# Laying out anew the filler products of a kernel's last four modes

## The chip, the cores and the metric

The kernel runs on one core of one Trainium2 chip. The metric is the time of one execution on the device, in microseconds (us); lower is better. Times below are medians of several executions.

Engine names in the profile: PE stands for the matrix products (2551 `MATMUL` records in the kernel before), PEld for the loads of their stationary operand (as many `LDWEIGHTS`), DVE and ACT for the vector and scalar engines; POOL and SP here mostly start DMA transfers (161 of POOL's 165 records are `DMA_DIRECT2D`). "PEclk" is the clock granted to PE, as a share of the full one. L340 is line 340 of the kernel. In the changed kernel lines from 381 on stand two lower, so L404 before is L406 after.

## The reference

A linear attention forms `x`. A spectral mix then takes the first 64 Fourier modes of `x` along the sequence, multiplies each mode by its own complex 512x512 matrix and transforms back. A channel product with a rectifier ends it:

```python
X  = np.fft.rfft(x, axis=1)                       # x: (8, 576, 512)
Yr = einsum(Xr, w_r) - einsum(Xi, w_i)            # per mode m: "bmd,mde->bme", 64 modes
Yi = einsum(Xr, w_i) + einsum(Xi, w_r)
y  = np.fft.irfft(Y, n=S, axis=1)
u  = x + y
out = u + np.maximum(u @ w_ch, 0.0)
```

What matters for the time: each mode has two weight matrices (`wr`, `wi`), 128 in all, which are loaded once and used once.

## The kernel before

The weights come in mode by mode. Each mode `kk` multiplies `wr`, then `wi` into a PSUM tile `P`; DVE or ACT casts `P` to `ys`; four small products turn it into `yt`. In the last four modes (60 to 63) *fillers* are put in: products of the identity with part of `wch16` into a PSUM tile that nobody reads before it is overwritten. They only keep PE at work. `pin` fixes the order in the program.

```python
    def w_load(kk, half, pool, tag, bufs):
        # ... the last weight, wi of mode 63, comes in two transfers: 3/4 and 1/4
        for dcs in (slice(0, 3), slice(3, 4)) if (kk, half) == (NM - 1, 1) else (slice(0, NDC),):
            tc.keep_in_program_order(nc.gpsimd.dma_start(out=w[:, dcs], in_=rows_of[:, dcs, :]))

    def keep_warm(n):
        for _ in range(n):
            pin(nc.tensor.matmul(last_ps[0], id16, wch16[:, 0, :]))      # 128x512, L340

    def mode_product(kk, ps, stage, yt_ps):
        # ...
        for t, w in ((1, wr), (0, wi)):
            # ... four products of 32 columns each, side by side, into P           (L355)
            if t == 1 and kk >= NM - 4:
                keep_warm(6)                       # first place: between wr and wi
        if NM - 4 <= kk < NM - 1:
            keep_warm(3)                           # second place: while P is cast
        # ... ys = cast of P: DVE in even modes (L369), ACT in odd ones (L371)
        # ... yt = four products of ys with pick_sb                                (L373)
        if NM - 4 <= kk < NM - 1:
            keep_warm(3)                           # third place: after yt

    def last_mode(ps):                             # mode 63, 16 products per weight (L393)
        # ...
        product(1, wr, range(NDC))
        keep_warm(3)
        product(0, wi, range(3))
        product(0, wi, range(3, NDC))
        nc.vector.tensor_copy(out=YT[:, :, kk, :], in_=y_last)          # "the YT cast", L404
```

After the YT cast come the products `zl` and `ypl` (L674, L684), small transfers into `YZ`, and a tail of inverse products (L549, L593) with the stores of the output.

Of the kernel before, what the change touches and what calls it, by code (L numbers as in the profile page):

```python
# [47 lines left out]
def kernel(  # L48
# [48 lines left out]
    def xt_cols(dc: int, t: int, kk: int):  # L97

        c0 = dc * XDC + t * B * NM + kk
        return xt_c[:, c0 : c0 + 31 * NM + 1 : NM]  # L100
# [231 lines left out]
    def w_get(kk: int):  # L332
        if kk not in w_in:
            w_in[kk] = [w_load(kk, half, wpool, "w", W_KEEP) for half in range(2)]
        return w_in.pop(kk)

    def keep_warm(n: int):

        for _ in range(n):
            pin(nc.tensor.matmul(last_ps[0], id16, wch16[:, 0, :]))  # L340

    def mode_product(kk: int, ps, stage, yt_ps):

        wr, wi = w_get(kk)
        st = stage.tile([128, D], F16, tag="ystage", bufs=2, name=f"ys{kk}")

        n_part = 1
        pw = D // n_part
        P = [
            ps.tile([128, D], F32, tag="P", bufs=2, name=f"P{kk}_{i}")[:, 0:pw] for i in range(n_part)  # L350
        ]
        for t, w in ((1, wr), (0, wi)):
            for i in range(n_part):
                for dc in range(NDC):
                    mm = nc.tensor.matmul(  # L355
                        P[i][dc * 32 : dc * 32 + 32, :], xt_cols(dc, t, kk),
                        w[:, dc, i * pw : i * pw + pw],
                        start=(t == 1), stop=(t == 0), tile_position=(0, dc * 32),
                    )
                    if kk >= NM - 4:  # L360
                        pin(mm)
            if t == 1 and kk >= NM - 4:
                keep_warm(6)
        if NM - 4 <= kk < NM - 1:
            keep_warm(3)
        for i in range(n_part):
            dst = st[:, i * pw : i * pw + pw]
            if (kk + i) % 2 == 0:
                nc.vector.tensor_copy(out=dst, in_=P[i])  # L369
            else:  # L370
                nc.scalar.copy(out=dst, in_=P[i])  # L371
        for ec in range(NDC):
            mm = nc.tensor.matmul(  # L373
                yt_ps[:, ec, kk % 8, :], st[:, ec * 128 : ec * 128 + 128], pick_sb
            )
            if kk >= NM - 4:
                pin(mm)
        if NM - 4 <= kk < NM - 1:
            keep_warm(3)

    def last_mode(ps):

        kk = NM - 1
        wr, wi = w_get(kk)
        y_last = ps.tile([128, NDC, 2 * B], F32, tag="P", bufs=2, name="y_last")

        def product(t, w, dcs):
            for dc in dcs:
                c0 = dc * XDC + t * B * NM + kk
                x = xt_c[:, c0 : c0 + (2 * B - 1) * NM + 1 : NM]  # L390
                for ec in range(NDC):
                    pin(
                        nc.tensor.matmul(  # L393
                            y_last[:, ec, :], w[:, dc, ec * 128 : ec * 128 + 128], x,
                            start=(t == 1 and dc == 0 and ec == 0), stop=(t == 0 and dc == NDC - 1),
                            skip_group_check=True,
                        )
                    )

        product(1, wr, range(NDC))  # L400
        keep_warm(3)
        product(0, wi, range(3))
        product(0, wi, range(3, NDC))
        nc.vector.tensor_copy(out=YT[:, :, kk, :], in_=y_last)  # L404
# [23 lines left out]
    def mode(kk: int):  # L428
        nonlocal yt_ps
        if kk % 8 == 0:  # L430
            yt_ps = psW.tile([128, NDC, 8, 2 * B], F32, tag="yt", bufs=1, name=f"yt{kk // 8}")
        if kk == NM - 1:
            last_mode(psW)
            return
        mode_product(kk, psW, ystage, yt_ps)
        if kk == NM - 2:
            nc.vector.tensor_copy(out=YT[:, :, NE : NM - 1, :], in_=yt_ps[:, :, 0 : NL - 1, :])
        elif kk % 8 == 7:
            nc.vector.tensor_copy(out=YT[:, :, kk - 7 : kk + 1, :], in_=yt_ps)
# [299 lines left out]
```

## Time and profile before

The median was 431.39 us of three runs (431.38 to 431.8).

| quantity | value | where it is read |
|---|---|---|
| span of the profiled execution | 429.8 us | page |
| queue of the weights (with q, k and v) | 82 MB, 98.2% of the DMA engines' span | page, queues |
| PE clock | 0.50 or 1.00 by turns, then 1.00 from 364.2 to 425.6 us | windows, clock records |
| fillers | 39 | code, timeline |
| last YT cast starts | 395.68 us | timeline |
| last piece of `wi` of mode 63 lands | 380.74 + 13.8 = 394.5 us | DMA issues |
| YT cast to the end of the span | 34.1 us | 429.77 - 395.68 |

From the page of the kernel before: the rows of the PE's busy share and of its clock in 40 slices of 10.7 us (tenths), the queue of the weights, and the chain that ended last.

```profile
PE   0358776887018776856886666778675758999993
PEclk9999666565558765566556678555658655999998
q0 software_dynamic: 32000, 82.00, 98.2%
DMA 67%; PE 17%; issue 7%; DVE 4%; ACT 2%; POOL 1%; DVEq 0%; POOLq 0%; ACTq 0%
```

Two thirds of the chain is waiting for transfers, 55% for weights (`wi` 33%, `wr` 22% in the page's list by line). PE is mostly under 80% busy until about slice 35, and its clock is low on average. Then the last slices are full and at full clock: PE takes over there. The change lies in that stretch.

From the timeline of the kernel before (start us, duration us, engine, line, operation, out<-in, shape, count, and in brackets the idle time before it with its releaser), mode 60 and then mode 63:

```profile
380.20 1.07 POOL L115 DMA_DIRECT2D wi<-in_moe_w_i_dram  x2
...
382.25 0.47 PE L355 MATMUL P<-wr,xt_c 128*32 128x512 bf16 x4
382.66 1.47 PE L340 MATMUL zl<-wch,id 128*128 128x512 f16 x6
384.06 0.47 PE L355 MATMUL P<-wi,xt_c 128*32 128x512 bf16 x4
384.47 0.82 PE L340 MATMUL zl<-wch,id 128*128 128x512 f16 x3
384.59 0.69 DVE L369 CAST ys<-P 128x512 f16<-128x512 f32 x1 [5.18 <-PE P L355]
385.33 0.26 PE L373 MATMUL yt<-pick_sb,ys 128*128 128x16 f16 x4
385.45 0.81 PE L340 MATMUL zl<-wch,id 128*128 128x512 f16 x3
386.19 0.47 PE L355 MATMUL P<-wr,xt_c 128*32 128x512 bf16 x4
...
393.68 0.73 PEld L393 LDWEIGHTS <-wr 128*128 128x128 bf16 x16
394.36 0.81 PE L340 MATMUL zl<-wch,id 128*128 128x512 f16 x3
394.80 0.73 PEld L393 LDWEIGHTS <-wi 128*128 128x128 bf16 x16
395.68 0.22 DVE L404 CAST YT<-y_last 128x64 f16<-128x64 f32 x1 [1.64 <-PE y_last L393]
395.97 1.05 PE L674 MATMUL zl<-wch,YT 128*128 128x256 f16 x8 [0.32 <-DVE YT L404]
```

No line of PE between 382 and 395 us carries an idle bracket: PE is never waiting for a weight here. The three fillers in the second place (384.47) run in the very time that the DVE cast takes (384.59 to 385.28), before `yt` can start at 385.33. The other fillers are followed at once by the next real product, so they push it back. The first line shows that the last weights were already under way at 380.2 us. From the view of DMA issues of the kernel before, window around 380.7 us (size, us from issue to landing), the two pieces of `wi` of mode 63:

```profile
wi<-in_moe_w_i_dram POOLq DMA_DIRECT2D x1, 384.0 KB, 13.6
wi<-in_moe_w_i_dram POOLq DMA_DIRECT2D x1, 128.0 KB, 13.8
```

Issued at 380.20 and 380.74 us, they land at 393.8 and 394.5 us. PE starts to load that weight at 394.80, so it is 1.0 us late for the first piece.

### The profile page before, as it was taken

Reading aid. Unit: us, or ns where it says so; the run is one execution under the profiler, and the core shown is the slowest. Engines: PE = TensorE matmul, PEld = TensorE weight load, DVE = VectorE, ACT = ScalarE, POOL = GpSimd, SP = SyncE. Lnnn points to the kernel's source line nnn. Section 1 sums busy time; section 2 is a strip of 40 time slices with the busy share of each in tenths; the row PEclk is TensorE's granted clock in tenths of the full one; section 3 lists DMA queues with packets and bytes.
Section 4 is the critical chain, followed back from the end, with each engine's and each line's share of the span. In section 5 each row is a group of like instructions: output and inputs, shape, how many; then the busy total and the mean of one; then the engine's idle time right before and its main releaser. Section 6 shows DMA issues by size and latency. Waiting matters only on the chain.

```text
span 429.8 us, 6238 instructions
## 1 busy us (share of the span) xinstructions
PE 296.9 (69%) x2551; PEld 154.8 (36%) x2551; DVE 181.9 (42%) x373; ACT 146.6 (34%) x227; POOL 91.5 (21%) x165
## 2 busy tenths in 40 slices
PE   0358776887018776856886666778675758999993
PEld 0346555664003332322232222322222324954441
DVE  1699998955004233233232322332323322211694
ACT  3687666631002222222222322122212222311782
POOL 4232223222102312121112221221211121110200
PEclk9999666565558765566556678555658655999998
DMA  8999999999999999999999999999999999995697
GB/s 148 207 208 209 209 210 210 211 214 215 222 211 214 215 213 214 214 214 214 213 213 214 214 213 214 213 214 214 213 213 214 214 214 214 214 213 97 239 369 296
DMA packets 35803, 92.38 MB, mean 215 GB/s; under 512 B 3136, under 2 KB 16448, under 8 KB 35776
## 3 DMA queue, kind: packets, MB, share of 16 engines
q0 software_dynamic: 32000, 82.00, 98.2%
q1 hardware_dynamic: 3776, 10.00, 6.1%
q8 instruction: 20, 0.33, 0.3%
q14 instruction: 7, 0.06, 0.0%
HBM read 164.07 MB, written 9.44 MB: 404 GB/s over the span
## 4 chain that ended last, share of the span: by engine, by line
DMA 67%; PE 17%; issue 7%; DVE 4%; ACT 2%; POOL 1%; DVEq 0%; POOLq 0%; ACTq 0%
DMA wi<-in_moe_w_i_dram 33%; DMA wr<-in_moe_w_r_dram 22%; DMA k<-in_k_dram 11%; PE acc L549 4%; PE P L355 3%; PE z L530 2%; PE zl L340 2%; PE acc L593 2%; PE eps L507 2%; PE yp L534 1%; DVE x L272 1%; ACT ke L187 1%; DVE k L194 0%; ACT qT L223 0%; POOL q L169 0%
## 5 line engine op out<-in xcount | busy, mean ns | idle before, releaser
L507 PE MATMUL eps<-wch,xTw 128*128 128x512 f16 x144 | 62.3, 582 | 3.4 <-DVE xTw L504 3.1
L515 ACT CAST E<-eps 128x512 f16<-128x512 f32 (+1 forms) x40 | 21.3, 543 | 122.7 <-PE eps L507 122.7
L115 POOL DMA_DIRECT2D wr<-in_moe_w_r_dram x64 | 34.0, 531 | 135.5 <-PE P L355 109.4
L355 PE MATMUL P<-wi,xt_c 128*32 128x512 bf16 x252 | 42.1, 565 | 27.3 <-DMA wi<-in_moe_w_i_dram 27.3
L355 PE MATMUL P<-wr,xt_c 128*32 128x512 bf16 x252 | 42.6, 582 | 22.9 <-DMA wr<-in_moe_w_r_dram 20.9
L115 POOL DMA_DIRECT2D wi<-in_moe_w_i_dram x65 | 34.5, 531 | 108.5 <-PE P L355 74.1
L355 PEld LDWEIGHTS <-xt_c 128*32 128x32 bf16 x504 | 24.3, 163 | 67.8 <-issue 38.7
L369 DVE CAST ys<-P 128x512 f16<-128x512 f32 x32 | 22.0, 688 | 59.7 <-PE P L355 59.7
L151 PEld LDWEIGHTS <-qT 64*128 64x128 f16 (+1 forms) x640 | 21.5, 126 | 56.8 <-issue 41.8
L371 ACT CAST ys<-P 128x512 f16<-128x512 f32 x31 | 18.1, 585 | 63.2 <-PE P L355 63.0
L373 PE MATMUL yt<-pick_sb,ys 128*128 128x16 f16 x252 | 16.8, 177 | 31.6 <-DMA pick_sb<-row_pick 20.4
L504 DVE COPY xTw<-xTp 128x512 f16<-128x512 f16 x36 | 15.2, 423 | 51.8 <-PE xTp L502 51.8
L373 PEld LDWEIGHTS <-ys 128*128 128x128 f16 x252 | 12.3, 105 | 51.1 <-issue 23.4
L151 PE MATMUL num<-kv,qT 64*128 64x65 f16 (+1 forms) x320 | 14.0, 230 | 22.6 <-ACT kv L247 20.1
L507 PEld LDWEIGHTS <-xTw 128*128 128x128 f16 x144 | 14.7, 124 | 33.7 <-issue 24.2
L492 DVE TENSOR_TENSOR x_main<-nw,rd 128x256 f32<-128x256 f32 x32 | 12.1, 419 | 33.8 <-PE nw L151 33.7
L187 ACT ACTIVATE qe<-q 128x1152 f16<-128x1152 f16 x16 | 17.7, 1155 | 22.9 <-DMA q<-in_q_dram 22.9
L216 PE MATMUL qTp<-id,qe 128*128 128x128 f16 x144 | 16.6, 310 | 12.1 <-DVE qe L200 11.7
L499 ACT CAST x16w<-x_main 128x512 f16<-128x512 f32 x32 | 19.8, 619 | 14.2 <-DVE x_main L492 14.2
L272 DVE TENSOR_TENSOR x<-num,rd 128x512 f16<-128x512 f32 x32 | 22.1, 691 | 1.1
L491 DVE RECIPROCAL rdw<-nw 128x4 f32<-128x4 f32 (+1 forms) x40 | 5.5, 170 | 38.3 <-PE nw L151 38.2
L502 PE MATMUL xTp<-id,x16w 128*128 128x128 f16 x144 | 19.4, 278 | 2.8 <-ACT x16w L499 2.4
(71 smaller groups left out, 413.7 us busy)
## 6 DMA issues: line engine op xcount, KB each, us to landing
wr<-in_moe_w_r_dram POOLq DMA_DIRECT2D x64, 512.0 KB, 18.6
wi<-in_moe_w_i_dram POOLq DMA_DIRECT2D x63, 512.0 KB, 18.6
out_dram<-x_main SPq DMA_DIRECT2D x14, 512.0 KB, 3.1
q<-in_q_dram POOLq DMA_DIRECT2D x8, 576.0 KB, 13.5
k<-in_k_dram POOLq DMA_DIRECT2D x8, 576.0 KB, 14.7
v<-in_v_dram POOLq DMA_DIRECT2D x8, 576.0 KB, 16.9
out_dram<-x_main SPq DMA_DIRECT2D x4, 256.0 KB, 3.4
out_dram<-x_tail SPq DMA_DIRECT2D x2, 512.0 KB, 3.4
```

What stands on the lines that cost most here:

```text
L115: tc.keep_in_program_order(nc.gpsimd.dma_start(out=w[:, dcs], in_=rows_of[:, dcs, :]))
L151: mm = nc.tensor.matmul(num[hpo][orow, c0 : c0 + 65], qT[rows, hpp, h2, cols], kv_sb[rows, hpp, h2, :])
L187: pin(nc.scalar.activation(out=ev[:, c], in_=heads(nm, b)[:, c], func=AF.Exp))
L272: nc.vector.tensor_tensor(out=dst.rearrange("p (o c d) -> p o c d", o=2, c=4), in0=nv[:, :, :, 0:64], in1=rden.unsqueeze(3).broadcast_to([ ...
L355: mm = nc.tensor.matmul(P[i][dc * 32 : dc * 32 + 32, :], xt_cols(dc, t, kk), w[:, dc, i * pw : i * pw + pw], start=(t == 1), stop=(t == 0) ...
L369: nc.vector.tensor_copy(out=dst, in_=P[i])
L371: nc.scalar.copy(out=dst, in_=P[i])
L373: mm = nc.tensor.matmul(yt_ps[:, ec, kk % 8, :], st[:, ec * 128 : ec * 128 + 128], pick_sb)
L499: nc.scalar.copy(out=x16, in_=x)
L502: nc.tensor.transpose(xT_ps[:, c, :], x16[:, c * 128 : c * 128 + 128], id16)
L507: nc.tensor.matmul(e_ps, xT[:, c, :], wch16[:, c, :], start=(c == 0), stop=(c == NDC - 1))
L515: nc.scalar.copy(out=dst, in_=e_ps[:, cols])
```

## The change

The intent, by its own words: fewer fillers in the first two of the four modes, and more between the last mode's two weight halves. The three numbers of a mode are the three places marked above; 39 fillers become 32.

```diff
             if t == 1 and kk >= NM - 4:
-                keep_warm(6)
+                keep_warm(FILL[kk][0])
         if NM - 4 <= kk < NM - 1:
-            keep_warm(3)
+            keep_warm(FILL[kk][1])
 ...
         if NM - 4 <= kk < NM - 1:
-            keep_warm(3)
+            keep_warm(FILL[kk][2])
+
+    FILL = {60: (3, 1, 1), 61: (5, 2, 2), 62: (6, 3, 3), 63: (6, 0, 0)}
 ...
         product(1, wr, range(NDC))
-        keep_warm(3)
+        keep_warm(FILL[kk][0])
         product(0, wi, range(3))
```

In this form the kernel before is `60, 61, 62: (6, 3, 3), 63: (3, 0, 0)`. The order of instructions on every engine other than PE is the same in both.

## The prediction

> **What bounds the kernel now.** The page's chain is 67% DMA: the stream of weights (98% of the 16 engines' span on the software queue) sets the time up to about 361 us. Windows view and timeline show a switch there: from 361 to 397 us the PE hardly pauses, at full clock (PEclk 1.00 from 364.2 to 425.6 us), first on a backlog (z, yp), then from 382.25 us on modes 60 to 63 with 39 fillers (L340). The chain in this stretch runs through PE, except for casts. DMA issues (start plus time to landing) against the timeline: wr60 377.2, used 382.25; wr61 382.1, used 386.2; wr62 387.0, used 390.1; wr63 392.0, used 393.7; first three quarters of wi63 393.8, used 394.8; last quarter 394.5, used about 395.3. Slack shrinks from 5 to under 1 us.
>
> **What the change does.** Only PE's order changes: ten fillers leave before mode 63 (mode 60: 3, 2, 2; mode 61: 1, 1, 1), three join between wr63 and wi63; 32 remain. Weights are issued before 381 us, ahead of the first filler, so landings should not move. One full-clock 128x512 product costs 0.215 us (chain: four take 0.86).
>
> - The three fillers taken between the wi products and yt are worth nothing: yt waits for the cast (DVE 0.69, ACT 0.58 us, plus handovers; 0.80 to 0.87 us from filler start to yt), longer than three fillers (0.65).
> - The other seven (3+1 before wi, 2+1 after yt) are on the chain: 7 x 0.215 = 1.5 us. Mode 63 then wants wr63 at about 392.2, just after its landing.
> - Three added fillers give back 0.65 us. wi63 is then wanted at about 393.95, its landing 393.8; the last quarter at about 394.45, its landing 394.5. A wait of 0.1 to 0.2 us may appear there.
>
> Net on the critical path: about -0.86 us by PE, at most about -0.8 by the landing of the last quarter; I take -0.7. Everything after should just slide earlier.
>
> **Clock.** [...] In the windows view, full-clock stretches of that length with 1.6 to 1.9 us of PE work are mostly followed by half clock; 2.67 and 2.71 us (377.9 and 394.9 us) are not. The thinned modes keep, by my estimate, at least 2.7 of 3.41 us. So I expect it to hold; lost before the tail, it would cost about 100 inverse products up to 0.2 us each.
>
> **Predicted time: 430.7 us (before 431.39), 80% range 430.1 to 431.6.** Chances: faster by over 2% 0.005, within 2% 0.97, slower by over 2% 0.025.
>
> **What would show it right:** first P product of mode 60 at the same time (about 382.3); mode 61 some 1.1 us earlier, mode 62 about 1.5 earlier; yt in mode 60 after 0.5 us of PE idle released by the cast; wi63 and the first zl (L674) 0.6 to 0.9 us earlier; PEclk still 1.00 up to the last products; the same distance from zl to the end.
>
> **What would make it wrong:** the landing of wr63 or wi63 releasing the last products later than I read (stragglers: DMA share is only 0.15 in the last 1.5 us), which would eat the gain; the clock dropping; a tail set by stores rather than by its start; noise (the runs before span 0.4 us).

The sum: 7 x 0.215 us off and 3 x 0.215 us on are the -0.86 us by PE, the landing makes it -0.8 at most, and -0.7 was taken. The 0.215 us is read from the trace: four products of 512 columns at full clock (L549) take 0.86 us from the first start to the next product's (403.33 to 404.19 us). "That length" is 3.41 us, the step in the windows view. Between 261.8 and 340.3 us five such stretches at full clock held 1.61 to 1.93 us of PE work; four were followed by half clock (1.61, 1.93, 1.76 and 1.83 us), one was not (1.88 us). That the clock would hold with 2.7 us is an inference from these and from the two stretches with 2.67 and 2.71 us. The 2.7 us itself is an estimate. The cost of a lost clock is an estimate too: at half clock four `eps` products of 512 columns took 1.68 us to the next product's start (360.70 to 362.38 us), 0.42 each, which is 0.2 us more than 0.215.

## The result, and the profile after

In the first measurement the changed kernel took 430.85 us (430.51 to 431.29, four runs) against 431.44 us (431.38 to 431.8, four runs). The ratio was 0.9985, with a 95% interval of 0.9968 to 1.0002: within 2%, and by itself not clear of 1. The experiments ran on four different chips, so kernels are compared through the ratio. A ratio is the mean time of one kernel's runs over that of the other's of the same rounds, so it isn't quite the ratio of the medians.

The timeline of the kernel after, the lines that answer to those of before:

```profile
379.46 1.07 POOL L115 DMA_DIRECT2D wi<-in_moe_w_i_dram  x2
...
381.51 0.47 PE L355 MATMUL P<-wr,xt_c 128*32 128x512 bf16 x4
381.92 0.82 PE L340 MATMUL zl<-wch,id 128*128 128x512 f16 x3
382.67 0.47 PE L355 MATMUL P<-wi,xt_c 128*32 128x512 bf16 x4
383.07 0.39 PE L340 MATMUL zl<-wch,id 128*128 128x512 f16 x1
383.20 0.69 DVE L369 CAST ys<-P 128x512 f16<-128x512 f32 x1 [4.53 <-PE P L355]
383.94 0.26 PE L373 MATMUL yt<-pick_sb,ys 128*128 128x16 f16 x4 [0.48 <-DVE ys L369]
384.06 0.38 PE L340 MATMUL zl<-wch,id 128*128 128x512 f16 x1
384.37 0.47 PE L355 MATMUL P<-wr,xt_c 128*32 128x512 bf16 x4
...
391.42 0.73 PEld L395 LDWEIGHTS <-wr 128*128 128x128 bf16 x16
392.10 1.46 PE L340 MATMUL zl<-wch,id 128*128 128x512 f16 x6
393.18 0.82 PEld L395 LDWEIGHTS <-wi 128*128 128x128 bf16 x16
394.16 0.23 DVE L406 CAST YT<-y_last 128x64 f16<-128x64 f32 x1 [2.37 <-PE y_last L395]
394.44 1.05 PE L676 MATMUL zl<-wch,YT 128*128 128x256 f16 x8 [0.32 <-DVE YT L406]
```

The two profiled executions differ by 1.53 us in span (429.77 against 428.24), which is more than the 0.86 us that the prediction gave the change at most. Their runs took 431.88 and 430.51 us, one above the median of its kernel and one below. The timelines split it. Mode 60 starts 0.74 us sooner (381.51 against 382.25), before any filler: that is a difference between executions, not of the kernels (more on it at the end). From there to the YT cast it takes 12.65 us instead of 13.43, 0.78 less: that belongs to the change. From the YT cast to the end of the span it takes 34.08 us against 34.09: nothing.

Inside the 0.78 us, mode 60 to 61 takes 2.86 us instead of 3.94. That is 1.08 less for five fillers in the chain (5 x 0.215 = 1.08), although seven have left. The other two stood in the second place; where they were, there is now a bracket of 0.48 us of idle time that ends with the cast. At the end, loading `wi` takes 0.82 instead of 0.73 us: about 0.1 us of waiting for its last piece.

### The profile page after: what moved, and what is told of

Same layout as the page of the kernel before. It is cut to its first block, busy times and chain, and to the rows that moved or that the text cites. A ratio compares the mean times of both kernels' runs of the same rounds, so it can differ in the third digit from the quotient of the medians.

```text
span 428.2 us, 6224 instructions
## 1 busy us (share of the span) xinstructions
PE 295.5 (69%) x2544; PEld 153.7 (36%) x2544; DVE 182.0 (42%) x373; ACT 146.7 (34%) x227; POOL 91.9 (21%) x165
## 4 chain that ended last, share of the span: by engine, by line
DMA 67%; PE 17%; issue 7%; DVE 4%; ACT 2%; POOL 1%; DVEq 0%; POOLq 0%; ACTq 0%
DMA wi<-in_moe_w_i_dram 33%; DMA wr<-in_moe_w_r_dram 23%; DMA k<-in_k_dram 11%; PE acc L551 4%; PE P L355 3%; PE z L532 2%; PE acc L595 2%; PE eps L509 2%; PE zl L340 2%; PE yp L536 1%; DVE x L272 1%; ACT ke L187 1%; DVE k L194 0%; ACT qT L223 0%; POOL q L169 0%
```

## The experiments

Every experiment is the changed kernel with other numbers in `FILL`, so each diff is one line (against the changed kernel), and all gave right results. Five measurements per profile tell most of it, so they come first as one table. "Mode 60" is the start of its first product, "landing" the issue of the last piece of `wi` of mode 63 plus its time to landing (good to 0.1 us), "YT" the start of the YT cast, all in us of the timeline. "Tail" is the span minus YT. The last two columns are the median of the timed runs and their ratio, not the profiled run alone. "Clock lost" is a stretch with PEclk 0.50 between 366 and 420 us.

| profile | mode 60 | landing | YT | YT - landing | tail | clock lost | time, us | ratio to before (95%) |
|---|---|---|---|---|---|---|---|---|
| before | 382.25 | 394.54 | 395.68 | 1.14 | 34.09 | no | 431.44 | |
| the change, first | 381.51 | 393.80 | 394.16 | 0.36 | 34.08 | no | 430.85 | 0.9985 (0.9968 to 1.0002) |
| same_again | 380.94 | 394.12 | 394.43 | 0.31 | 34.04 | no | 430.81 | 0.9979 (0.9967 to 0.9992) |
| again_b | 381.57 | 394.85 | 395.24 | 0.39 | 34.14 | no | 431.01 | 0.9991 (0.9975 to 1.0006) |
| cast_only | 381.64 | 394.12 | 395.07 | 0.95 | 34.20 | no | 431.89 | 0.9996 (0.9984 to 1.0009) |
| chain_only | 381.67 | 394.25 | 394.58 | 0.33 | 34.14 | no | 430.84 | 0.9979 (0.9966 to 0.9991) |
| add_only | 381.75 | 393.84 | 395.78 | 1.94 | 34.10 | no | 432.30 | 1.0016 (1.0002 to 1.0030) |
| cut_only | 381.20 | 393.69 | 394.03 | 0.34 | 34.18 | no | 431.20 | 0.9996 (0.9980 to 1.0012) |
| cut_d | 380.87 | 393.75 | 394.06 | 0.31 | 34.09 | no | 430.73 | 0.9985 (0.9970 to 1.0001) |
| none | 382.27 | 394.45 | 394.77 | 0.32 | 35.41 | 385.5 to 399.2 | 432.47 | 1.0020 (1.0008 to 1.0032) |
| late_only | 379.60 | 393.79 | 394.83 | 1.04 | 34.25 | 385.0 to 391.8 | 431.45 | 0.9989 (0.9976 to 1.0003) |

Where the last landing is what PE waited for, the YT cast starts 0.31 to 0.39 us after it. Where the number is larger, PE itself came late.

**Theory A**: seven fillers that stand in PE's chain leave and three come; the three in the second place are hidden behind the cast; the landing of the last weight is the floor. **Rivals**: B, the gain is only where the weight stream happened to stand in that run; C, every filler costs its 0.215 us wherever it stands; D, the fillers do nothing for the clock.

### The change itself again (same_again)

No edit.

> The changed kernel once more, in five rounds. D is the distance in the timeline from the first P product of mode 60 to the last YT cast (from y_last): 13.43 us before, 12.65 in the first profile of the change (-0.78). Theory A (seven fillers on PE's chain leave, three come, and the landing of the last quarter of wi63 takes back about 0.1): D again 12.6 to 12.75, ratio of times about 0.998. Rival B (the 0.6 us of the first result is only where the run's weight stream happened to stand): D varies by as much as the time does, and the ratio is within 0.0005 of 1.

The ratio came as A said, 0.9979, with an interval that excludes 1, so rival B falls by its second half. The distance D did not come as A said: it was 13.49 us, 0.84 more than in the first profile, as the first half of B had it. From the timeline of same_again:

```profile
380.94 0.48 PE L355 MATMUL P<-wr,xt_c 128*32 128x512 bf16 x4
...
391.65 0.65 PE L395 MATMUL y_last<-xt_c,wr 128*128 128x16 bf16 x16 [0.27 <-DMA wr<-in_moe_w_r_dram]
393.45 0.94 PE L395 MATMUL y_last<-xt_c,wi 128*128 128x16 bf16 x16
394.43 0.22 DVE L406 CAST YT<-y_last 128x64 f16<-128x64 f32 x1 [3.06 <-PE y_last L395]
```

Here PE reached mode 60 sooner while the weights landed later. PE waited 0.27 us for `wr` and about 0.3 us inside `wi` (0.94 us instead of 0.64), and the YT cast stands 0.31 us after the last landing. So D is not a property of the kernel once the landing binds. The distance from the landing is the better measure, and the table uses it.

### Only the fillers beside the cast leave (cast_only)

```diff
-    FILL = {60: (3, 1, 1), 61: (5, 2, 2), 62: (6, 3, 3), 63: (6, 0, 0)}
+    FILL = {60: (6, 1, 3), 61: (6, 2, 3), 62: (6, 3, 3), 63: (3, 0, 0)}
```

> Only the three fillers that stand between a mode's wi products and its yt products leave (mode 60: two, mode 61: one); 36 remain. Theory A: PE waits for the ys cast there anyway, so D stays 13.43 us (13.35 to 13.5), idle before yt about 0.5 us in mode 60 and 0.2 in mode 61, ratio 1.000. Rival C (every filler costs its 0.215 us): D 12.8, ratio 0.9985.

D was 13.43 us (395.07 - 381.64), as before to the last digit, and the ratio 0.9996 (its interval, from 0.9984, still holds C's 0.9985, so it is the trace that decides). From the timeline of cast_only, the `yt` products of modes 60 and 61:

```profile
384.72 0.26 PE L373 MATMUL yt<-pick_sb,ys 128*128 128x16 f16 x4 [0.48 <-DVE ys L369]
...
388.59 0.26 PE L373 MATMUL yt<-pick_sb,ys 128*128 128x16 f16 x4 [0.20 <-ACT ys L371]
```

The fillers turned into idle time, 0.48 and 0.20 us. Rival C falls.

### All of the change but that (chain_only)

```diff
-    FILL = {60: (3, 1, 1), 61: (5, 2, 2), 62: (6, 3, 3), 63: (6, 0, 0)}
+    FILL = {60: (3, 3, 1), 61: (5, 3, 2), 62: (6, 3, 3), 63: (6, 0, 0)}
```

> The change without its cut between wi products and yt: seven fillers leave elsewhere, three come between wr63 and wi63; 35 remain. Theory A: the same as the change, D 12.65 us (12.55 to 12.75), ratio about 0.998. Rival C: D 0.65 us longer, 13.3, ratio about 0.9995.

The ratio was 0.9979, the same as the change's in the same rounds (medians 430.84 and 430.81 us). D was 12.91 us, above the range that was expected, because the landing bound it: YT came 0.33 us after the landing. From the timeline of chain_only, the last quarter of `wi` and the YT cast:

```profile
394.25 0.17 PEld L395 LDWEIGHTS <-wi 128*128 128x128 bf16 x4 [0.24 <-DMA wi<-in_moe_w_i_dram]
394.58 0.23 DVE L406 CAST YT<-y_last 128x64 f16<-128x64 f32 x1 [2.62 <-PE y_last L395]
```

Rival C predicted 0.9995, outside the interval (0.9966 to 0.9991), and falls here too.

### Only the three added (add_only)

```diff
-    FILL = {60: (3, 1, 1), 61: (5, 2, 2), 62: (6, 3, 3), 63: (6, 0, 0)}
+    FILL = {60: (6, 3, 3), 61: (6, 3, 3), 62: (6, 3, 3), 63: (6, 0, 0)}
```

> Only the three fillers between wr63 and wi63 are added; 42 in all. Theory A: they stand on the chain, no landing hides them (wi63 has landed 1 us before it is used), so D is 13.43 + 0.65 = 14.08 us, ratio about 1.0015. Rival (fillers there are hidden behind the landing of wi63): D stays 13.43, ratio 1.000.

D was 14.03 us, 0.60 more than before, and the ratio 1.0016. From the timeline of add_only, `wi` is loaded without a wait:

```profile
394.94 0.69 PEld L395 LDWEIGHTS <-wi 128*128 128x128 bf16 x16
395.78 0.22 DVE L406 CAST YT<-y_last 128x64 f16<-128x64 f32 x1 [2.23 <-PE y_last L395]
```

Added to a kernel whose PE is late, fillers between `wr` and `wi` cost nearly their full time (three times 0.215 is 0.65). In the change they are nearly free only because the other removals have made PE early.

### Only the ten removed (cut_only, cut_a, cut_b, cut_c, cut_d and again_b)

```diff
-    FILL = {60: (3, 1, 1), 61: (5, 2, 2), 62: (6, 3, 3), 63: (6, 0, 0)}
+    FILL = {60: (3, 1, 1), 61: (5, 2, 2), 62: (6, 3, 3), 63: (3, 0, 0)}
```

> The change's ten removals without its three additions; 29 fillers. Theory A: PE comes to wi63 0.65 us sooner than in the change but must wait for its landing: the first three quarters land about 0.7 us before the last one, so PE idles about 0.5 us before wi63 and again before its last quarter; D 12.55 to 12.65, no more than 0.1 below the change, ratio to before about 0.998. Rival (the landing isn't the floor, PE alone counts): D 12.0, ratio 0.9965. The clock stays at 1.00.

From the timeline of cut_only:

```profile
393.05 0.94 PE L395 MATMUL y_last<-xt_c,wi 128*128 128x16 bf16 x16 [0.43 <-DMA wi<-in_moe_w_i_dram]
394.03 0.23 DVE L406 CAST YT<-y_last 128x64 f16<-128x64 f32 x1 [2.53 <-PE y_last L395]
```

PE now waits twice for `wi`, 0.43 us for its first piece and about 0.3 us for the last, and YT comes 0.34 us after the landing, as in the change (0.36). D was 12.83 us, not 12.0, and above the range that was expected, because the landing came later after mode 60 (12.49 us) than in the first profile (12.29). So the landing is the floor, and in this profile taking more fillers away bought nothing. But the timed runs fell in two groups: 430.54, 430.65 and 430.77, and 431.64, 432.31 and 432.66 us.

> The kernel of cut_only again, one look. Its timed runs fell in two groups (430.5 to 430.8 and 431.6 to 432.7 us), the profiled one in the first. Theory A: the long group is executions in which the clock is lost for a stretch at the last mode, because PE waits there for wi63[...]; then a profile of a run over 431.6 us shows PEclk 0.50 somewhere between 388 and 400 us and a distance from the last YT cast to the end longer than 34.2 us, and a profile of a run under 430.9 shows 1.00 throughout and 34.0 to 34.2. Rival: the long group comes from a later landing of the weights; then the clock is 1.00 and the last landing stands 1 us later.

> As cut_a: one more look at the same kernel[...]. Theory A and its rival as there.

> As cut_a: one more look at the same kernel[...]. Theory A and its rival as there.

The three took 430.71, 431.33 and 430.46 us. The clock stayed at 1.00 to the tail in all three, and YT stood 0.37 to 0.39 us after the landing. In the longest one (cut_b) the last landing came at 394.50 us, against 394.04 and 393.81 in the other two: the landing made most of the difference, as the rival of these runs had it. Between cut_b and cut_c the span differs by 1.02 us, the landing by 0.69; 0.32 lie in the tail, which was 33.87, 34.19 and 33.87 us in cut_a, cut_b and cut_c. I had expected 34.0 to 34.2 for the short ones; why the tail was shorter wasn't looked into. Five more rounds, with the change beside it:

> The kernel of cut_only in five more rounds, side by side with the change itself (again_b). Four looks at it so far had the clock at 1.00 to the end and followed the last landing. If the three long runs of its first rounds (431.6 to 432.7 us) belong to the kernel (a clock lost at the last mode in some executions, by theory A), some of these runs are over 431.6 us again and its ratio to before stands at least 0.001 above that of again_b. If they were chance of that call, its runs lie in 430.4 to 431.4 us and the two ratios agree within 0.0007.

> The change itself once more, in the same rounds as cut_d: runs in 430.4 to 431.4 us, ratio to before 0.998 (0.997 to 0.999); in its profile the last YT cast starts 0.3 to 0.4 us after the last landing of wi63 if PE comes early, more if it comes late, and 34.0 to 34.2 us lie between that cast and the end.

This time cut_d's runs lay between 430.38 and 431.43 us and its ratio (0.9985) was as good as the change's (0.9991, just outside the 0.997 to 0.999 that I expected). The long group did not come back. The profile of again_b, the changed kernel, fell on a long run by chance: 431.6 us, over the range that was expected of its runs. From its timeline:

```profile
390.01 0.45 PE L355 MATMUL P<-wi,xt_c 128*32 128x512 bf16 x4 [0.29 <-DMA wi<-in_moe_w_i_dram]
...
392.45 0.65 PE L395 MATMUL y_last<-xt_c,wr 128*128 128x16 bf16 x16 [0.26 <-DMA wr<-in_moe_w_r_dram]
...
394.26 0.94 PE L395 MATMUL y_last<-xt_c,wi 128*128 128x16 bf16 x16
```

PE waited for three weights one after another; the last landing was at 394.85 us, the latest of all profiles, with the clock at 1.00 and a tail of 34.14 us. So a long run of this kernel can be one in which the weights came late. The runs over 432 us of cut_only were not profiled. The latest landing seen goes with a time of 431.6 us and not with those, so their cause stays open. A lost clock isn't excluded for them: in cut_d the 3.41 us from 392.89 us held only 2.39 us of PE work, less than any such stretch of the change between 376 and 400 us (2.58 at the least, in same_again and again_b). In cut_d the clock stayed at 1.00; in none, below, it was at 0.50 after a stretch with 1.97 us.

### No fillers at all (none)

```diff
-    FILL = {60: (3, 1, 1), 61: (5, 2, 2), 62: (6, 3, 3), 63: (6, 0, 0)}
+    FILL = {60: (0, 0, 0), 61: (0, 0, 0), 62: (0, 0, 0), 63: (0, 0, 0)}
```

> All 39 fillers leave. Without a clock effect D could fall no lower than the landing of wi63, about 12.6 us, as in the change. Theory A with the clock: PE has about 1 us of work in each 3.4 us while it waits for wr62 to wi63 (387 to 394.5 us), less than the 1.6 to 1.9 us after which the clock fell elsewhere in the trace, so the clock falls to 0.50 before wi63 and the first inverse products run at half speed[...]: D 13.0 to 14, the tail 2 to 4 us longer, ratio to before 1.003 to 1.008. Rival D (fillers do nothing for the clock here): PEclk stays 1.00, D 12.6, ratio 0.998.

From the windows of none, cut every 3.41 us so that the two changes of its clock fall on a cut (window, length, busy us and count of PE, PEld, DVE, ACT and POOL, then PEclk, DMA share, GB/s):

```profile
378.71:382.12 3.41, 2.67 (x22) 1.25 (x21) 0.42 (x1) 0.80 (x2) 1.70 (x4) 1.00 1.07 215
382.12:385.54 3.42, 1.97 (x22) 0.82 (x20) 0.69 (x1) 0.42 (x1) 0.00 (x0) 1.00 1.07 216
385.54:388.95 3.41, 0.96 (x8) 0.41 (x9) 0.00 (x0) 0.17 (x1) 0.00 (x0) 0.50 1.07 214
...
395.78:399.19 3.41, 3.23 (x14) 1.59 (x13) 0.42 (x1) 1.98 (x5) 0.92 (x2) 0.50 0.02 5
399.19:402.60 3.41, 3.41 (x17) 1.78 (x16) 1.80 (x3) 1.34 (x4) 1.98 (x5) 1.00 0.46 147
```

After a window with 1.97 us of PE work the clock was at half, and it came back only at 399.2 us, after a window with 3.23 us. These are single observations and give no limit: one stretch of the kernel before (from 323.24 us) held 1.88 us of PE work, and the clock was still at 1.00 after it. The "about 1 us of work in each 3.4 us" of the expectation was an estimate; the three stretches from 385.54 to 395.78 us held 0.96, 1.31 and 1.76 us. Two lines of the timeline of none show how long PE paused before the clock fell, and what the fall cost:

```profile
383.76 0.26 PE L373 MATMUL yt<-pick_sb,ys 128*128 128x16 f16 x4 [0.79 <-DVE ys L369]
...
395.05 1.89 PE L676 MATMUL zl<-wch,YT 128*128 128x256 f16 x8 [0.32 <-DVE YT L406]
```

The first ends the longest idle time of PE in the window after which the clock fell, 0.79 us; no longer pause stands in it. In the second the `zl` products took 1.89 us instead of 1.05, and the tail was 35.41 us instead of 34.1. The landing was still the floor (YT 0.32 us after it). So in this profile 39 fillers are worth 1.3 us of tail, and rival D falls. I had expected 2 to 4 us and a ratio of 1.003 to 1.008; it was 1.0020. The direction was right, the size was not.

### Fillers only in the last two modes (late_only)

```diff
-    FILL = {60: (3, 1, 1), 61: (5, 2, 2), 62: (6, 3, 3), 63: (6, 0, 0)}
+    FILL = {60: (0, 0, 0), 61: (0, 0, 0), 62: (6, 3, 3), 63: (6, 0, 0)}
```

> No fillers in modes 60 and 61; mode 62 as it was and six between wr63 and wi63; 18 remain. PE waits about 1 us for wr62. Theory A: the landing of wi63 is the floor as in the change (last YT cast 0.3 to 0.4 us after that landing); whether the clock holds is the question: if it does in all runs the ratio to before is 0.998 and the tail 34.1 us; if the idle of modes 60 and 61 costs the clock before the late fillers win it back, some runs are 0.5 to 2 us longer and the ratio is 0.999 to 1.003. Rival (only the fillers just ahead of the tail matter): 0.998 with a spread no wider than the change's.

From the timeline of late_only:

```profile
386.37 0.69 PE L355 MATMUL P<-wr,xt_c 128*32 128x512 bf16 x4 [0.98 <-DMA wr<-in_moe_w_r_dram]
386.99 2.74 PE L340 MATMUL zl<-wch,id 128*128 128x512 f16 x6
389.66 0.68 PE L355 MATMUL P<-wi,xt_c 128*32 128x512 bf16 x4
```

The clock was lost at 385.0 us, and the six fillers ran at half of it: 2.67 us from their start to the next product, against 1.40 in the kernel before (382.66 to 384.06). The clock was back at 1.00 from 391.8 us, so the tail was whole (34.25 us), but PE came 0.7 us late for the last weight (YT 1.04 us after the landing instead of about 0.35). My expectation that the landing would still be the floor was wrong: I had priced the fillers at full clock. In this profile late fillers alone were dearer than fillers spread out. The timed runs can't tell: the ratio, 0.9989 (0.9976 to 1.0003), fits theory A's slower case and does not exclude the rival's 0.998, and the five runs lie as close together (431.13 to 431.55 us) as the rival asked.

No version beat the change clearly. chain_only equals it; its five runs were the closest together of all (430.71 to 430.97 us).

## Why the prediction was right

- **The bound and the cost of a filler: right.** In the kernel before, only PE and the casts stand between mode 60 and the YT cast; 5 x 0.215 us foretold what left between modes 60 and 61 to 0.01 us (1.08). Mode 62 starts 6.29 us after mode 60 instead of 7.81, 1.52 less; I had said about 1.5.
- **The fillers beside the cast: right**, and shown by cast_only (D unchanged) and chain_only (same time as the change).
- **The three added fillers: right.** add_only lengthened D by 0.60 us; three times 0.215 is 0.65.
- **The landing as the limit: right in kind, too narrow in size.** "A wait of 0.1 to 0.2 us may appear there" held in the first profile (0.1). But I took the landing as fixed against PE's work. Over the profiles the last landing came 11.98 us (cut_c) to 13.28 us (again_b) after the start of mode 60, and 14.19 us in late_only, whose mode 60 started earliest of all. In same_again and again_b the waits came to 0.9 and 1.1 us (D 13.49 and 13.67, against 13.43 - 4 x 0.215 = 12.57 by PE alone). In such an execution the kernel before would have met the same floor: 13.28 + 0.35 = 13.63 us is more than its own 13.43. So the gain of one execution lies, by this estimate, anywhere from nothing to 0.86 us.
- **The sum: right.** I took -0.7 us. The medians of the first measurement differ by 0.59. The mean of the three ratios of the change (0.9985, 0.9979, 0.9991) is 0.9985, or 0.65 us of 431.4. That one call came so near to my number is in part luck: only one of the three intervals of the change excludes 1, and -0.7 lies between executions in which the landing takes hardly anything from the 0.86 us and others in which, by the estimate above, it takes all.
- **"The first P product of mode 60 at the same time (about 382.3)": wrong.** It came at 381.51, and anywhere from 379.60 (late_only) to 382.27 (none) in the profiles. This moves D from one profile to the next by as much as the change does. The traces point to the clock: mode 60 starts earlier where the last rise of the clock to 1.00 before it, with which PE worked off its backlog of `z` and `yp` products, came earlier. That rise stood at 357.7 us in late_only (mode 60 at 379.60), 362.2 in cut_d (380.87), 363.4 in the first profile of the change (381.51), 364.2 before (382.25) and 365.1 in none (382.27); over all fourteen profiles the correlation is 0.94, and 0.85 without late_only. No experiment tested this.
- **The clock: right.** I had estimated at least 2.7 us of work in 3.41 us in the thinned modes; in the first profile of the change the two stretches there (380.47 to 387.30 us) had 3.00 and 3.14, and the clock held at 1.00. Where the fillers were really missing (none), it fell to 0.50 at 385.5 us, which shows that the risk I named was a real one.

## What to carry to other kernels

In this kernel fillers that keep PE's clock up are free only where PE would wait anyway, for a cast or for a transfer; elsewhere each costs its full duration (0.215 us at full clock), and more once the clock is already lost (2.67 us for six in late_only, against 1.40 before). So put them just ahead of the wait that really binds, here the landing of the last weight, and take them out where they delay the work that is wanted next, as long as the clock holds until then (in late_only it did not). When a gain is a tenth of a per cent, split the two timelines at a fixed instruction and at the last landing rather than compare spans: of 1.53 us between two profiles here, half had nothing to do with the change.
